# Removing the branch prefetch hints ahead of the jump over a fallback path

## The chip, the cores and the metric

The kernel runs on one core of one Trainium2 chip. The metric is the device time of one execution in microseconds. The profile's span, from the first to the last instruction, is about 1.8 us shorter than that time (342.1 us against 343.89 us for the profiled execution of the kernel before).

In the profile's lines PE is TensorE, PEld its weight loads, ACT ScalarE, DVE VectorE, POOL GpSimd and SP SyncE; a "q" behind the name means the engine's instruction sequencer, and L706 is line 706 of the kernel.

## The reference

The reference computes two independent problems A and B of attention with a cached K and V and concatenates their results. Each has 16 batches, 32 query tokens, 32 query heads on 4 key/value heads and 512 cached keys:

```python
q = (x @ wq).reshape(B, Sq, Hq, Dh)...            # 512 x 1024 times 1024 x 4096
scores = einsum("bhqd,bhkd->bhqk", q, k) * (Dh ** -0.5)
p = softmax(scores, axis=-1)
o = einsum("bhqk,bhkd->bhqd", p, v)
a = o.reshape(B, Sq, Hq * Dh) @ wo                # and b the same with the B inputs
return concatenate([a, b], axis=-1)
```

## The kernel before

The fast path takes the softmax with a constant shift in place of each row's maximum. That is good only while all row sums stay in a safe range, so VectorE counts at the end how many sums do. Every engine loads that count into a register and, if it is too small, runs a slower general path that recomputes everything. On the given inputs the count is full: **the general path is never executed, and every engine jumps over it.**

```python
            run(units, 40)                      # 40 steps of the last output projections
            tc.mark_branch_hint_location(       # what the change removes
                "general", "LikelyTaken",
                [nc.sync.engine, nc.scalar.engine, nc.vector.engine, nc.tensor.engine, nc.gpsimd.engine],
            )
            ok = nc.values_load(ok_i[0:1, 0:1], ...)      # line 670: one register load per engine
            run(units, 1 << 20)                 # the rest of the output projections
            return ok
    ...
    ok = fast_path(ok_i)
    with tc.If(ok < total, preferred_fallthrough_block=True, label="general"):   # line 679
        general_path(tc, problems, out_flat)
```

The program that this builds has, for each engine, the fast path, a compare-and-branch, then the general path (578 instructions on ScalarE, 844 on VectorE, 266 on GpSimd, 7,811 on PE, one on SyncE), then a short else block of semaphore updates, then the closing barriers. The branch is taken, to the else block. The last output piece is cast by ScalarE and stored by a DMA that ScalarE issues:

```python
                yield from f_units(1, TT - 1, 0, NW, nc.sync)
                yield from f_units(1, TT - 1, NW, QW, nc.sync)
                yield from f_units(1, TT - 1, NW + QW, QW, nc.scalar)   # the last piece
```

## Time and profile before

| | before |
|---|---|
| time, median (lowest to highest) of the first 3 runs | 343.97 us (343.52 to 344.53) |
| span of the profiled execution | 342.1 us |
| PE busy | 338.1 us |
| start of the last cast; from there to the end | 339.09 us; 3.0 us |

The page of the profile gives the span, the engines' busy times and the chain of work that ended last:

```profile
span 342.1 us, 5510 instructions
PE 338.1 (99%) x2128; PEld 214.6 (63%) x2128; DVE 265.6 (78%) x336; ACT 185.7 (54%) x209; POOL 46.6 (14%) x206
...
PE 99%; ACT 0%; issue 0%; ACTq 0%
```

TensorE bounds the kernel. The windows view splits the span where the last cast starts. The columns are the stretch, its length, the busy time of PE, PEld, DVE, ACT and POOL, the granted clock, the DMA share and GB/s; the last stretch was asked for 0.1 us past the end of the span:

```profile
0.00:339.09 339.09, 338.08 (x2128) 214.64 (x2128) 265.55 (x336) 185.35 (x208) 46.65 (x206) 1.00 0.87 211
339.09:342.20 3.11, 0.00 (x0) 0.00 (x0) 0.00 (x0) 0.37 (x1) 0.00 (x0) 1.00 0.08 24
```

The last 3 us hold one cast and nothing else that counts as busy. The hints themselves appear in the view of the kernel's last source line, to which the compiler attributes them (duration in ns as minimum/median/maximum, then the start of the first and the last in us):

```profile
L706 POOLq BRANCH_PREFETCH_HINT  x1: 56/56/56, 0.7 to 0.7; - x1
L706 ACTq BRANCH_PREFETCH_HINT  x1: 50/50/50, 0.7 to 0.7; - x1
L706 SPq BRANCH_PREFETCH_HINT  x1: 60/60/60, 0.7 to 0.7; - x1
L706 DVEq BRANCH_PREFETCH_HINT  x1: 51/51/51, 0.8 to 0.8; - x1
L706 PEldq BRANCH_PREFETCH_HINT  x1: 50/50/50, 0.8 to 0.8; - x1
```

They run at 0.7 to 0.8 us, at the very start, though the source marks them near the end. The branches appear in the view of the If's line. An engine's EVENT_SEMAPHORE on that line is its first instruction behind the jump:

```profile
L679 POOLq EVENT_SEMAPHORE  x5: 17/43/43, 331.0 to 331.4; - x5
L679 POOLq COMPARE_BRANCH  x1: 64/64/64, 330.6 to 330.6; - x1
L679 DVEq COMPARE_BRANCH  x1: 84/84/84, 330.6 to 330.6; - x1
L679 DVEq EVENT_SEMAPHORE  x1: 21/21/21, 331.2 to 331.2; - x1
...
L679 PEldq COMPARE_BRANCH  x1: 402/402/402, 336.9 to 336.9; - x1
L679 PEldq EVENT_SEMAPHORE  x1: 51/51/51, 339.1 to 339.1; - x1
L679 ACTq COMPARE_BRANCH  x1: 68/68/68, 339.9 to 339.9; - x1
L679 ACTq EVENT_SEMAPHORE  x1: 17/17/17, 340.4 to 340.4; - x1
```

ScalarE is the last to branch, at 339.9, and goes on half a microsecond later. GpSimd and VectorE have branched 9 us earlier. SyncE closes the program: it waits for all engines and stores. Its own waits on the kernel's last line, from 335 us on (what it waited for, us in total, times, longest):

```profile
...
SPq L706 <- DMA out_dram<-o_sb: 2.0, 1, 2.0
SPq L706 <- PEq L679: 1.9, 1, 1.9
...
```

Its last long wait ended when the last store landed. ScalarE's part of the job was done by then.

### The profile page before, as it was taken

What the parts mean: (1) busy time and instruction counts of PE and PEld (TensorE: products, weight loads), DVE (VectorE), ACT (ScalarE), POOL (GpSimd) and SP (SyncE); (2) the same over time, 40 slices, a digit from 0 to 9 for tenths busy, and PEclk for the clock granted to TensorE, in tenths of its full rate; (3) what the DMA queues carried; (4) which work ended last, traced back from release to release, by engine and by line L of the source; (5) the groups of instructions that cost most, each with busy time, mean ns of one, the idle gap of its engine ahead of it and who ended that gap; (6) DMA issues with size and microseconds to landing.
All of it is one profiled execution on the core that took longest, in us unless ns stands there. A gap on an engine that the chain in (4) does not pass through costs nothing.

```text
span 342.1 us, 5510 instructions
## 1 busy us (share of the span) xinstructions
PE 338.1 (99%) x2128; PEld 214.6 (63%) x2128; DVE 265.6 (78%) x336; ACT 185.7 (54%) x209; POOL 46.6 (14%) x206
## 2 busy tenths in 40 slices
PE   8999999999999999999999999999999999999996
PEld 7456666666666666666666666666666666666555
DVE  1047988888888889888888888798888888889540
ACT  2067666676666666676655554555454555555110
POOL 0001111101111111111101212222122100111100
DMA  6999999899999998999999856999439996430001
GB/s 194 253 243 183 284 261 256 173 232 269 299 234 248 238 252 231 251 304 303 281 319 259 191 125 180 283 323 211 129 104 306 350 194 139 103 96 17 17 17 33
DMA packets 128093, 71.70 MB, mean 210 GB/s; under 512 B 75840, under 2 KB 127296, under 8 KB 128064
## 3 DMA queue, kind: packets, MB, share of 16 engines
q1 hardware_dynamic: 127536, 70.21, 84.7%
q0 software_dynamic: 384, 1.05, 0.9%
q8 instruction: 17, 0.28, 0.3%
q14 instruction: 12, 0.10, 0.1%
q10 hardware_dynamic: 144, 0.07, 0.1%
HBM read 50.86 MB, written 2.10 MB: 155 GB/s over the span
## 4 chain that ended last, share of the span: by engine, by line
PE 99%; ACT 0%; issue 0%; ACTq 0%
PE f_ps L320 32%; PE q_ps L301 28%; PE ob L425 16%; PE s_ps L357 16%; PE q_ps L533 4%; PE q_ps L515 1%; PE xT_ps L523 0%; ACT o_sb L329 0%; ACTq L329 0%
## 5 line engine op out<-in xcount | busy, mean ns | idle before, releaser
L365 ACT ACTIVATE p_sb<-s_ps,shift 128x1024 bf16<-128x1024 f32 x128 | 142.6, 1114 | 97.8 <-PE s_ps L357 82.0
L376 DVE TRANSPOSE_TENSOR_REDUCE parts<-p_sb 128x32 f32<-128x1024 bf16 x128 | 158.8, 1240 | 19.2 <-ACT p_sb L365 17.6
L320 PE MATMUL f_ps<-wo_sb,oT 128*128 128x512 bf16 (+1 forms) x544 | 131.8, 366 | 0.0
L301 PE MATMUL q_ps<-xT,wq_sb 128*128 128x512 bf16 x448 | 117.4, 379 | 0.0
L425 PE MATMUL ob<-p_sb,v_sb 128*128 128x256 bf16 x512 | 76.8, 273 | 0.0
L357 PE MATMUL s_ps<-qT,kT 128*128 128x256 bf16 x512 | 76.8, 273 | 0.0
L320 PEld LDWEIGHTS <-oT 128*128 128x128 bf16 x544 | 53.2, 98 | 35.8
L357 PEld LDWEIGHTS <-kT 128*128 128x128 bf16 x512 | 56.9, 113 | 28.3
L301 PEld LDWEIGHTS <-wq_sb 128*128 128x128 bf16 x448 | 43.8, 98 | 31.7 <-DMA wq_sb<-in_A_wq_dram 0.2
L425 PEld LDWEIGHTS <-v_sb 128*128 128x128 bf16 x512 | 50.1, 98 | 20.0
L447 DVE TENSOR_TENSOR oT<-r,ob 128x512 bf16<-128x512 f32 x64 | 43.9, 686 | 21.9 <-PE ob L425 20.8
L411 DVE STREAM_TRANSPOSE r<-rall 128x512 f32<-128x512 f32 x64 | 44.2, 691 | 1.1
L309 ACT CAST qT<-q_ps 128x512 bf16<-128x512 f32 x56 | 32.6, 583 | 15.4 <-PE q_ps L301 15.4
L394 POOL COPY half<-cs 64x32 f32<-64x32 f32 x32 | 6.5, 204 | 227.4 <-DVE cs L384 227.3
L329 ACT CAST o_sb<-f_ps 128x512 bf16<-128x512 f32 (+1 forms) x17 | 9.5, 558 | 24.6 <-PE f_ps L320 24.6
L533 PE MATMUL q_ps<-xT,w_sb 128*128 128x512 bf16 (+1 forms) x70 | 15.4, 377 | 0.0
L384 DVE TENSOR_REDUCE cs<-parts 128x32 f32<-128x128 f32 x32 | 12.0, 376 | 1.1
L406 DVE RECIPROCAL rall<-sums 128x32 f32<-128x32 f32 x32 | 10.2, 320 | 3.3 <-POOL sums L403 3.3
L533 PEld LDWEIGHTS <-w_sb 128*128 128x128 bf16 x70 | 7.2, 104 | 6.9
L561 DVE CAST qT<-q_ps 128x512 bf16<-128x512 f32 x4 | 2.5, 683 | 10.2 <-PE q_ps L533 10.2
L331 POOL DMA_DIRECT2D out_dram<-o_sb x8 | 4.6, 574 | 34.7 <-ACT o_sb L329 34.6
L395 POOL TENSOR_TENSOR half<-half,cs 64x32 f32<-64x32 f32 x32 | 7.8, 242 | 2.6
(25 smaller groups left out, 46.3 us busy)
## 6 DMA issues: line engine op xcount, KB each, us to landing
v_sb<-in_A_v_cache_dram SPq DMA_DIRECT2D x16, 512.0 KB, 6.5
wq_sb<-in_B_wq_dram SPq DMA_DIRECT2D x8, 1024.0 KB, 6.0
wo_sb<-in_A_wo_dram SPq DMA_DIRECT2D x8, 1024.0 KB, 6.4
v_sb<-in_B_v_cache_dram SPq DMA_DIRECT2D x16, 512.0 KB, 4.4
wo_sb<-in_B_wo_dram SPq DMA_DIRECT2D x8, 1024.0 KB, 8.4
wq_sb<-in_A_wq_dram SPq DMA_DIRECT2D x5, 1024.0 KB, 6.3
wq_sb<-in_A_wq_dram SPq DMA_DIRECT2D x2, 512.0 KB, 5.8
kT<-in_A_k_cache_dram SPq DMA_TRANSPOSE x64, 4.5
```

What stands on the lines that cost most here:

```text
L301: nc.tensor.matmul(ps[:], lhsT=w[:, dc, (h % 4) * DH:(h % 4 + 1) * DH], rhs=xT[pr][:, dc, :], start=(dc == 0), stop=(dc == DC - 1),)
L309: nc.scalar.copy(out=qT[pr, g][:, :, hl, :], in_=ps[:].rearrange("p (b s) -> p b s", s=SQ),)
L320: nc.tensor.matmul(ps[:, 0:width], lhsT=oT[pr, tt][:, h, :], rhs=wo_tiles[pr, nh, h // REP][:, h % REP, off:off + width], start=(h == 0), ...
L357: nc.tensor.matmul(s_ps[:, c, :], lhsT=kT[:, i % GRP, c, :], rhs=qT[pr, g][:, b, :, :].rearrange("p h s -> p (h s)"), start=True, stop=True,)
L365: nc.scalar.activation(out=p_sb[:], in_=s_ps[:], func=ACTF.Exp, bias=shift[:], scale=SCALE)
L376: nc.vector.tensor_reduce(out=parts[k][:, q, :, :].rearrange("p c h -> p (c h)"), in_=st[i]["p"][:].rearrange("p c (h s) -> p (c h) s", s=SQ),
L384: nc.vector.tensor_reduce(out=cs[:], in_=parts.pop(k)[:].rearrange("p q c h -> p q h c"), axis=AX.X, op=ALU.add,)
L406: nc.vector.reciprocal(out=rall[:, k, :], in_=quad.pop(k)[:])
L411: nc.vector.transpose(out=r[:].rearrange("p n s -> p (n s)"), in_=rall[:, k, o * 2 * REP:(o + 1) * 2 * REP] .unsqueeze(2).to_broadcast([P, ...
L425: nc.tensor.matmul(ob[j][:, q, :], lhsT=v_sb[:, i % GRP, c, :], rhs=st[i]["p"][:, c, :], start=(c == 0), stop=(c == KC - 1),)
L447: nc.vector.tensor_tensor(out=out, in0=rcp.pop(j)[:].rearrange("p (q h) s -> p q h s", h=REP), in1=ob.pop(j)[:].rearrange("p q (h s) -> p ...
L533: nc.tensor.matmul(first_q[h][:, ts], lhsT=w0[dc // HC][:, dc % HC, h * DH:(h + 1) * DH], rhs=xT[0][:, dc, ts], start=(dc == 0 and t0 == 0 ...
```

## The change

By its name a hint is to have the instructions at the jump's target fetched before the jump. The change takes all five away. Its whole text is:

```diff
             run(units, 40)
-            tc.mark_branch_hint_location(
-                "general",
-                "LikelyTaken",
-                [nc.sync.engine, nc.scalar.engine, nc.vector.engine, nc.tensor.engine, nc.gpsimd.engine],
-            )
             ok = nc.values_load(ok_i[0:1, 0:1], min_val=0, max_val=total,
```

## The prediction

> **What bounds the kernel.** TensorE. The profile page gives PE 338.1 us busy of a 342.1 us span, and the chain that ended last is 99% PE. The windows view of 339.10 to 342.20 shows no PE work at all: the last 3 us are a tail in which ScalarE casts the last output piece (339.09, 0.37 us), issues its output DMA (339.49, 0.38 us), takes the compare-and-branch over the general path (339.90) and meets the other engines in the closing barriers (last record 342.05). The change touches only this tail and the kernel's first microsecond.
>
> **What the change removes.** One BRANCH_PREFETCH_HINT per engine. By the records of the kernel's last source line they do not stand where the source marks them but at 0.70 to 0.82 us, 50 to 60 ns each, ahead of SyncE's first load (0.857) and PE's first matmul (0.93). Removing them starts both some 0.06 to 0.1 us earlier: about -0.07 us.
>
> **What it adds.** The program's branch is taken (the data passes the check), over a general path of 578 ScalarE, 844 VectorE, 266 GpSimd and 7,811 PE instructions, but one SyncE instruction. [...] The trace of before[...]: from the start of the branch to the next instruction take 0.49 us (GpSimd 330.55 to 331.05), 0.61 (VectorE), 0.48 (ScalarE 339.90 to 340.39), 0.20 (SyncE), and the instruction-fetch records come only after that, 0.60 to 0.62 us after the first target instruction (331.67, 331.83, 340.98). So the targets were already there, which I put down to the hints[...].
>
> Without hints each of the four engines must fetch at the branch. Estimate from these records: about 0.1 us to decide, 0.6 to 0.9 us until the fetch starts, 0.55 us for an 8 KB fetch (PE: 16 KB, 1.1 us), [...]0.4 us to resume: about 2.2 to 2.5 us, so 1.7 to 2 us more than now; I allow 1.2 to 3.
>
> **How much is on the critical path.** GpSimd and VectorE branch at 330.6: 10 us of slack, nothing. PE's sequencer branches at 336.90 and then waits for its own matmuls until 339.05: a 2.5 to 4 us stall gives 339.4 to 340.9, still before the end. [...] ScalarE's branch counts: its end event moves from 340.40 to about 342.2. SyncE now goes on at 341.14, released by the landing of the last output DMA, so about 0.7 us of the stall is hidden behind that transfer; the rest delays the closing barriers one for one. Net: +1.8 - 0.7 - 0.07, about +1.1 us, with +0.3 to +2.6 possible.
>
> **Predicted time.** 345.1 us, range 344.2 to 346.6. Chances: faster by over 2% 0.01, within 2% 0.97, slower by over 2% 0.02.
>
> **What would show it.** No hint records at 0.7 us. In the records of the If line, the gap from ScalarE's COMPARE_BRANCH to its next event grows from 0.48 to about 2.3 us; likewise VectorE and GpSimd, not SyncE. Two instruction fetches after each branch, the first before the engine resumes. SyncE's last wait of the tail is released by ScalarE, not by the output DMA. PE's busy time unchanged at 338.1; the span grows by as much as the time.
>
> **What would make it wrong.** A fetch quick enough to hide in the 0.7 us (then no change); a hint that never worked, the target being present for another reason (then -0.07); a PE stall over 4 us, PE then ending last; or a run-to-run spread (343.52 to 344.53 before) that covers it.

Four things are cut from it, as no trace of this case shows them: a rule for when a jump has to wait for its target, with the words that refer to it; how the hints were thought to have had the targets ready; one term of the stall's estimate, which rests on no record; and where SyncE's target lies. The stall came to 2.2 to 2.5 us in the author's sum. The terms as first written add up to 1.95 to 2.25 us, and those that are left to 1.65 to 1.95 us.

## The result, and the profile after

| | before | after |
|---|---|---|
| time, median (lowest to highest) of 6 runs each | 343.94 us (343.42 to 344.53) | 345.06 us (344.70 to 346.21) |
| ratio, 95% interval | | 1.0037 (1.0019 to 1.0055) |
| span of the profiled execution | 342.1 us | 344.4 us |
| PE busy | 338.1 us | 338.5 us |
| start of the last cast; from there to the end | 339.09; 3.0 us | 339.68; 4.7 us |

A ratio is the mean time of one kernel's fast runs over that of the other's of the same rounds, so it is not quite the ratio of the medians. Here the means are 345.16 and 343.89 us, a difference of 1.27 us. The verdict at 2% is "same"; at this resolution the kernel is slower by about a third of a per cent. The profiled execution of after was the slowest of its six.

The windows view of after, split at its last cast:

```profile
0.00:339.68 339.68, 338.46 (x2128) 214.75 (x2128) 265.53 (x336) 185.34 (x208) 46.66 (x206) 1.00 0.87 211
339.68:344.50 4.82, 0.00 (x0) 0.00 (x0) 0.00 (x0) 0.37 (x1) 0.00 (x0) 1.00 0.07 20
```

Of the 2.3 us by which this span is longer, 0.6 lie ahead of the last cast and 1.7 behind it. Part of the 0.6 has nothing to do with the branch: PE waited 0.4 us for a late weight tile at 72 us, as it does for 0.2 to 0.8 us in the traces of e4, e6, e7 and e9. The If's line in after (five source lines higher, as the call is gone):

```profile
L674 POOLq EVENT_SEMAPHORE  x5: 17/43/43, 333.7 to 334.1; - x5
L674 POOLq COMPARE_BRANCH  x1: 45/45/45, 331.1 to 331.1; - x1
L674 DVEq COMPARE_BRANCH  x1: 72/72/72, 331.2 to 331.2; - x1
...
L674 DVEq EVENT_SEMAPHORE  x1: 21/21/21, 334.2 to 334.2; - x1
...
L674 PEldq COMPARE_BRANCH  x1: 3335/3335/3335, 337.5 to 337.5; - x1
L674 ACTq COMPARE_BRANCH  x1: 54/54/54, 340.5 to 340.5; - x1
L674 PEldq EVENT_SEMAPHORE  x1: 51/51/51, 340.9 to 340.9; - x1
L674 ACTq EVENT_SEMAPHORE  x1: 17/17/17, 343.4 to 343.4; - x1
```

Four engines now stand still for 2.6 to 3.3 us at the branch. On PE the stall is inside the branch's own record (3,335 ns against 402); on the others it is the gap behind it. SyncE's waits from 335 us on:

```profile
SPq L701 <- PEq L674: 3.2, 1, 3.2
SPq L701 <- ACTq L674: 2.5, 1, 2.5
...
```

SyncE is now released by ScalarE (ACTq) and no longer by the store. To the nanosecond, from the raw instruction and fetch records of the two traces (us from the span's start):

```
                                       before      after
ScalarE issues the last store          339.494     340.085
ScalarE compare-and-branch             339.904     340.497
fetch of instructions starts, length      -        341.703, 0.307
ScalarE's first instruction behind it  340.388     343.432
last store landed, SyncE sees it       341.141     341.735
SyncE sees ScalarE's event (wait ends) 341.169     343.478
last instruction ends                  342.104     344.411
```

In before, ScalarE's event (it ends at 340.405) comes 0.74 us ahead of the landing. In after, its event (343.449) comes 1.71 us behind the landing. The branch gap grew from 0.484 to 2.935 us, that is by 2.45 us; 0.74 us of it is hidden behind the store, and 1.71 us stick out. That is the whole growth of the tail.

### The profile page after: what moved, and what is told of

It is laid out like the page before. It is cut to its first block, busy times and chain, and to the rows that moved or that the text cites. A ratio compares the mean times of both kernels' runs of the same rounds, so it can differ in the third digit from the quotient of the medians.

```text
span 344.4 us, 5505 instructions
## 1 busy us (share of the span) xinstructions
PE 338.5 (98%) x2128; PEld 214.8 (62%) x2128; DVE 265.5 (77%) x336; ACT 185.7 (54%) x209; POOL 46.7 (14%) x206
## 4 chain that ended last, share of the span: by engine, by line
PE 90%; SPq 6%; DMA 2%; issue 0%; ACT 0%; ACTq 0%
PE f_ps L320 32%; PE q_ps L301 23%; PE ob L425 15%; PE s_ps L357 15%; PE q_ps L533 4%; SPq L275 3%; DMA wq_sb<-in_A_wq_dram 2%; SPq L602 2%; PE q_ps L515 1%; PE xT_ps L523 0%; SPq L283 0%; SPq L246 0%; ACT o_sb L329 0%; ACTq L329 0%
```

## The experiments

The theories, as they stood before the runs:

- **S**: only ScalarE's stall reaches the end, because ScalarE issues the last store and branches last. Rival **P**: PE's stall, the longest, sets the end.
- **W**: the stall is the fetch of a target that is far from the branch; a near one needs none. Rival **F**: any taken branch without a hint pays a flat penalty. Rival **B**: for ScalarE a target behind half of the general path (289 or 290 instructions) is still near. Rival **M**: the stall belongs to a conditional branch gone the wrong way.
- **O**: the stall costs what sticks out past the landing of the last store, and no more.

Kernels are compared only within the same rounds.

"Gap" is the time from the start of an engine's branch to the start of its next instruction, from the raw records. "Tail" is the time from the start of ScalarE's last cast to the end of the span. Before has a tail of 3.01 us, after 4.73 us. All these kernels gave correct results.

### e1: ScalarE's hint alone

```diff
-                [nc.sync.engine, nc.scalar.engine, nc.vector.engine, nc.tensor.engine, nc.gpsimd.engine],
+                [nc.scalar.engine],
```

> Only ScalarE keeps its hint. Theory S (ScalarE's stall at the branch, 2.94 us in the trace of after against 0.48 before, is all that reaches the end): ScalarE's branch gap back to 0.4 to 0.5 us; PE's branch record stays 3.3 us long, VectorE and GpSimd gaps about 3.0 and 2.6 us, all hidden; SyncE's last wait released by the output DMA again; first load at 0.74 us as in after. Time 343.7, that is before minus 0.1 to 0.2 us. Rival P (PE's stall, the longest, 3.3 us, sets the end): time stays about 1.1 us above before, 345.1.

Measured: ratio 0.9995 (0.9982 to 1.0008); median 343.59 us against 343.57 for before. The tail is 3.01 us. From the view of the If's line:

```profile
L679 PEldq COMPARE_BRANCH  x1: 3318/3318/3318, 336.6 to 336.6; - x1
L679 ACTq COMPARE_BRANCH  x1: 68/68/68, 339.6 to 339.6; - x1
L679 PEldq EVENT_SEMAPHORE  x1: 51/51/51, 340.0 to 340.0; - x1
L679 ACTq EVENT_SEMAPHORE  x1: 17/17/17, 340.1 to 340.1; - x1
```

PE stalls 3.3 us, GpSimd and VectorE 2.62 and 2.97 us, and it costs nothing: the tail is that of before to 0.01 us. ScalarE's hint is worth all that the five are worth.

### e2: all hints but ScalarE's

```diff
+                [nc.sync.engine, nc.vector.engine, nc.tensor.engine, nc.gpsimd.engine],
```

> All engines but ScalarE keep the hint. Theory S: ScalarE's gap about 2.9 us, the other four as before, first load at 0.86 us as before; time 1.2 to 1.7 us above before, 345.3 (a little over after, since the hints' issue slots at the start are paid and nothing is gained). Rival P: time as before, 343.9.

Measured: ratio 1.0045 (1.0031 to 1.0058), means 1.55 us apart; tail 4.58 us; ScalarE's gap 2.79 us, the others as in before (0.49, 0.61, 0.20 us, PE's record 402 ns). SyncE's longest wait:

```profile
SPq L706 <- ACTq L679: 3.6, 1, 3.6
```

With e1 this settles S against P for this layout of the program. PE is not far behind, though: in e1 it comes out of its branch at 339.95 us, 0.9 us ahead of the landing of the last store. Here the growth of the tail (1.57 us) and the difference of the means (1.55 us) agree.

### e3 and e4: half of the general path, and a stub of it, without hints

None of e3 to e6 is a correct kernel for all inputs, as the fallback is incomplete; all give correct results on these, where it isn't executed.

```diff
 # e3
-        general_path(tc, problems, out_flat)
+        general_path(tc, problems[:1], out_flat)
 # e4: the same, and eight loops inside general_path cut to one or two turns
```

> No hints; the general path (never executed on these inputs) handles one problem only: 290 ScalarE, 424 VectorE, 134 GpSimd, 3,907 PE instructions to jump over instead of 578, 844, 266, 7,811. Theory W[...]: GpSimd's [...]gap drops to about 0.5 us with no fetch before it resumes; ScalarE, VectorE and PE still stall 2.9, 3.0 and 3.3 us; time as after, 345.1. Rival F (any taken branch without a hint pays a flat penalty): GpSimd's gap stays 2.6 us. Rival B[...]: ScalarE's gap drops to 0.5 us as well and the time falls to 343.7.

> No hints; the general path cut to a stub (9 ScalarE, 14 VectorE, 19 GpSimd, 92 PE instructions), never executed on these inputs. Theory W: [...]no stall: gaps 0.2 to 0.6 us on all five, PE's branch record about 0.4 us, no target fetch; time before minus 0.1 to 0.2 us, 343.7. Rival F (flat penalty of an unhinted taken branch): gaps and time as after, 345.1.

Measured: e3 1.0115 (1.0100 to 1.0129), 3.9 us slower; e4 1.0027 (1.0014 to 1.0041), 0.9 us slower. Both times missed what was expected, e3's by far. The gaps did as theory W says: in e3 GpSimd 0.47, VectorE 2.93, ScalarE 2.56 us; in e4 GpSimd 0.18, VectorE 0.23, ScalarE 0.39, SyncE 0.19 us, PE's record 363 ns. What spoiled the times was the build. As the cut general path no longer writes problem B's part of the output, nothing ties the last store to the If, and the framework's builder put it behind the If (e5 and e6, whose stub still writes that part, kept it ahead). The timeline of ScalarE in e3 shows it:

```profile
338.72 0.37 ACT L329 CAST o_sb<-f_ps 128x256 bf16<-128x256 f32 x1 [3.12 <-PE f_ps L320]
341.43 2.06 ACTq L331 DMA_DIRECT2D out_dram<-o_sb  x1
```

The store now comes 2.7 us behind the start of the cast (0.40 in before), as it has to sit through the stall, and issuing it takes 2.06 us in place of 0.38, with one more instruction fetch inside (at 341.88 us). The tail is 7.0 us. In e4 the store slid behind the If too, but without a stall there, and the tail is 3.12 us. The rest of e4's 0.9 us lies ahead of the tail; in its trace PE waits 0.3 and 0.2 us for late tiles of v and wq. Why its six runs have more of that than others stays open.

### e5: half of the general path, the store kept in place

```diff
-        general_path(tc, problems, out_flat)
+        general_path(tc, problems[1:], out_flat)
```

> As e3, but the never executed general path keeps the problem whose output piece is stored last, so that store should stay ahead of the branch (in e3 it had slid behind it and cost time of its own). 289 ScalarE, 137 GpSimd, 3,907 PE instructions to jump over. Theory W: GpSimd's gap 0.5 us without a fetch first, ScalarE's 2.6 to 2.9 us with one, PE's record 3.3 to 3.7 us; time as after, 1.1 to 1.5 us above before. Rival B[...]: ScalarE's gap 0.5 us, time at most as before.

Measured: ratio 1.0034 (1.0014 to 1.0054), means 1.10 us apart; tail 4.65 us; gaps GpSimd 0.47, VectorE 2.83, ScalarE 2.86 us. From the view of the If's line:

```profile
L674 POOLq EVENT_SEMAPHORE  x5: 17/43/43, 330.3 to 330.6; - x5
L674 POOLq COMPARE_BRANCH  x1: 45/45/45, 329.8 to 329.8; - x1
...
L674 ACTq COMPARE_BRANCH  x1: 54/54/54, 339.1 to 339.1; - x1
...
L674 ACTq EVENT_SEMAPHORE  x1: 17/17/17, 342.0 to 342.0; - x1
```

In one and the same program, an unhinted taken branch over 137 instructions (GpSimd) takes half a microsecond and one over 289 (ScalarE) takes 2.9. These are two engines, but GpSimd alone says the same: over 266 instructions, in after, it took 2.59 us. So the distance matters, not the missing hint as such: F falls. B falls too: behind 289 instructions ScalarE's target was not near (2.86 us). Where between 8 and 289 instructions the limit lies for ScalarE was not measured.

### e6: a stub, the store kept in place

Edit: as e5, and eight loops of the general path cut to one or two turns (8 ScalarE, 19 VectorE, 30 GpSimd, 104 PE instructions).

> As e4, with the store of the last piece kept ahead of the branch: stub of 8 ScalarE, 19 VectorE, 30 GpSimd, 104 PE instructions. Theory W: no stall on any engine (gaps 0.1 to 0.4 us), SyncE's last wait released by the output DMA; from the last cast to the end 3.0 us as in before (4.7 in after); time 0 to 0.3 us under before. Rival F (flat penalty of an unhinted taken branch): ScalarE's gap 2.9 us, 4.7 us from the last cast to the end, time as after.

Measured: ratio 1.0004 (0.9982 to 1.0027); tail 2.98 us; gaps 0.18, 0.23, 0.19 and 0.19 us on GpSimd, VectorE, ScalarE and SyncE, and 363 ns for PE's record. No instruction fetch of GpSimd, VectorE or ScalarE follows the branches. SyncE's longest wait is for the store again:

```profile
SPq L701 <- DMA out_dram<-o_sb: 2.0, 1, 2.0
```

Without any hint, but with a near target, the tail is that of before. The 0 to 0.3 us under before that were expected don't show.

### e7: the last store issued by SyncE, no hints

```diff
-                yield from f_units(1, TT - 1, NW + QW, QW, nc.scalar)
+                yield from f_units(1, TT - 1, NW + QW, QW, nc.sync)
```

> No hints, full general path; the last output piece is stored by SyncE instead of ScalarE. Theory O (the stall costs only what sticks out past the landing of the last store): ScalarE's sequencer can take the branch as soon as its last cast is dispatched, 0.8 us earlier against that cast than in after, its stall stays 2.6 to 2.9 us, so the end comes 3.9 to 4.0 us after the start of the last cast instead of 4.7; time 0.6 to 0.8 us under after, 0.3 to 0.8 above before. Rival: the stall's length is what counts, wherever it starts: time as after.

Measured: ratio 1.0003 (0.9984 to 1.0022), means 0.28 us apart; tail 3.43 us. ScalarE's sequencer takes the branch 0.01 us after the start of the cast, against 0.81 us in after; its stall is 2.44 us; its event comes 0.4 us behind the landing of the store. The wait that is left for SyncE:

```profile
SPq L701 <- ACTq L674: 0.8, 1, 0.8
```

This bears O out. The expected tail (3.9 to 4.0 us) was too long, as the stall came out shorter than the 2.6 us assumed. It is 0.5 us shorter than in after, and it starts 0.8 us earlier against the cast, beside the issue and flight of the store, and the tail shrinks by 1.3 us: 0.8 for the earlier start and 0.5 for a shorter stall. This kernel needs no hint and comes within noise of before.

### e8: the else block placed first, no hints

```diff
-    with tc.If(ok < total, preferred_fallthrough_block=True, label="general"):
+    with tc.If(ok < total, preferred_fallthrough_block=False, label="general"):
```

> No hints, the If laid out so that the short else block falls through; that block then jumps over the general path to the end. Theory W: the compare-and-branch costs ScalarE 0.1 to 0.5 us and its end event comes at once, but the jump behind it stalls just the same (2.5 to 2.9 us until its drain), since its target is as far away: 4.5 to 4.7 us from the last cast to the end; time as after, 1.1 to 1.5 us above before. Rival M (the stall belongs to a mispredicted conditional branch): no stall, time 0 to 0.3 us under before.

Measured: ratio 1.0047 (1.0026 to 1.0069), means 1.57 us apart; tail 4.84 us. Each engine now has two branches; the second is the jump from the else block to the end.

```profile
L674 PEldq COMPARE_BRANCH  x2: 91/1931/3771, 336.4 to 338.7; - x2
L674 ACTq COMPARE_BRANCH  x2: 38/46/53, 339.4 to 339.6; - x2
...
L674 ACTq EVENT_SEMAPHORE  x1: 17/17/17, 339.5 to 339.5; - x1
```

And from the view of the kernel's last line, ScalarE's drain at the end:

```profile
L701 ACTq DRAIN  x2: 8/37/66, 342.2 to 342.8; - x2
```

The first, conditional one falls through in 0.10 us; PE's takes 91 ns. The second stalls: ScalarE's next instruction, its drain, comes at 342.24, 2.68 us later, and PE's record is 3,771 ns long. So M falls: it doesn't matter whether the branch that is far is the conditional one. Laying the If out the other way only moves the far jump. Two things were not expected, and with them the tail and the time came out a little above what was forecast (4.7 and 1.5 us). First, the last store took 3.1 us to land (1.6 in before and after). A 16 KB instruction fetch, taken for PE's (only one queue moves 16,384 bytes at a time, 17 times in before, where PE has 4,267 of the 5,510 recorded instructions), ran at 339.77 to 341.14, at the same time as that store (issued at 338.98), and the last eight packets of the store ran only from 341.13 on. That the two got into each other's way was not shown. Second, in this layout it is PE that ends last (a line of SyncE's waits, then one of the view of the kernel's last line):

```profile
SPq L701 <- PEq L701: 1.0, 2, 0.5
L701 PEldq DRAIN  x2: 8/40/73, 342.5 to 342.9; - x2
```

In after PE's far branch stood ahead of its wait for its own matmuls and began at 337.5; here the far jump stands behind that wait and begins at 338.69. PE's drain comes at 342.51, 0.3 us behind ScalarE's (342.24) and 0.4 behind the landing of the store (342.13). So which engine's stall sets the end depends on where its jump stands.

### e9, e10, e11: the small gain at the start

e9 is e1 again, e10 is after again; e11 takes away SyncE's hint alone:

```diff
+                [nc.scalar.engine, nc.vector.engine, nc.tensor.engine, nc.gpsimd.engine],
```

> The kernel of e1 once more, to see whether it beats before. ScalarE's hint alone should give the tail of before (3.0 us from the last cast to the end) with SyncE's first load at 0.74 instead of 0.86 us: 0.1 to 0.3 us under before, if the loads' own spread (0.5 us between runs) lets it be seen.

> The changed kernel once more, on the chip of e9 and e11: 4.6 to 4.8 us from the last cast to the end again (before: 3.0), whatever the loads do ahead of it; first load at 0.74 us; time 1.2 to 1.5 us over before, 1.4 to 1.7 over e9.

> All hints but SyncE's[...]. Branch gaps of all five as in before, 3.0 us from the last cast to the end; first load at 0.74 us as in after while PE still starts at 0.93. If what the hints cost at the start is SyncE's slot, time as e9; if PE's slot matters too, between e9 and before.

| | median us | ratio to before, 95% interval | tail us | first load at us |
|---|---|---|---|---|
| before, same rounds | 343.58 | | 3.01 (first trace) | 0.86 |
| e9, ScalarE's hint alone | 343.65 | 0.9993 (0.9979 to 1.0007) | 3.01 | 0.74 |
| e10, no hints (after) | 344.69 | 1.0028 (1.0015 to 1.0042) | 4.65 | 0.74 |
| e11, all hints but SyncE's | 343.40 | 0.9990 (0.9977 to 1.0004) | 3.02 | 0.74 |

The tails came as expected and the times of e10 lower than expected (0.98 us over before and 0.72 over e9 by the means, where 1.2 to 1.5 and 1.4 to 1.7 had been forecast). Two of e9's seven runs took 344.9 and 345.0 us, so that by the plain means of all runs it lies 0.27 us above before, though its ratio over the same rounds is below 1. Whether dropping the hints of engines that don't need them gains the 0.1 to 0.3 us that e9 was to show can't be told: all three intervals (e1, e9, e11) hold 1. No version was found that clearly beats both kernels.

## Why the prediction was right

- **The time.** Predicted 345.1 us (344.2 to 346.6); measured 345.06 us, and 344.69 us when repeated in e10. The mechanism was right; that the number agrees to 0.04 us is luck, as the mis-sized terms below show.
- **Which engine counts.** Predicted: ScalarE's branch only. Shown by e1 and e2: with its hint alone the tail is 3.01 us, with all hints but its own 4.58 us. The other three stalls are real (2.6, 3.0, 3.3 us in after) and hidden, as predicted. SyncE's gap was unchanged (0.20 and 0.19 us), as predicted.
- **Why it stalls.** Predicted: the target must be fetched at the branch. Shown by e5 and e6, where only the distance changed: over 8 instructions 0.19 us on ScalarE, over 289 2.86 us, over 578 2.94 us; and by an instruction fetch that starts and ends inside ScalarE's gap in every trace where that gap is long. In after it starts at 341.70 us, 1.21 us behind the start of the branch, and ends 1.42 us ahead of the next instruction.
- **The hidden part.** Predicted: about 0.7 us of ScalarE's stall disappears behind the landing of the last store. Measured: 0.74 us. Confirmed by e7, which hides more of it.
- **A term that was mis-sized: the stall.** It was put at 2.2 to 2.5 us; it is 2.94 us in after and 2.86 in e10. The terms as written add up to 1.95 to 2.25 us, without the one that is cut to 1.65 to 1.95 us. The transfer was about right (0.31 us in after, 0.68 in e5; put at 0.55). Too small were the ends: from ScalarE's branch to the start of the fetch 0.92 to 1.25 us over the traces (put at 0.7 to 1.0), and from the end of the fetch to the next instruction 1.08 to 1.42 us (put at 0.4 by the term that is left, at 0.7 with the cut one). So the tail grew by 1.72 us and not by 1.1.
- **The other mis-sized term: the start.** It was put at -0.07 us. SyncE's first load starts 0.12 us earlier (0.74 against 0.86) and PE 0.15 us earlier (0.78 against 0.93). The time of after grew by 0.45 us less than its tail (1.27 against 1.72), that of e10 by 0.66 us less (0.98 against 1.64). These two errors of the estimate have opposite signs, and that is why its sum came out so well. Where the 0.45 to 0.66 us come from is not settled. It may be noise: e6 and e7 start without hints too, and their time grew by 0.14 us more and by 0.14 us less than their tail. The start of the last cast lay anywhere between 338.3 and 340.2 us in the 13 traces, as PE waited for some late tile or not; e11, which moves only the first load, came out 0.29 us under before by the means, with a ratio whose interval holds 1.
- **How the hint had done it.** The records show this much: in before no 8 KB instruction fetch stands between the one that starts at 289.1 us and the first branch at 330.6 us, and yet GpSimd, VectorE and ScalarE were at their next instruction 0.48 to 0.61 us after the branch, ahead of any such fetch (331.67, 331.83 and 340.98 us). In the two traces with SyncE's hint (before and e2) there are 9 fetches of 8 KB between 5 and 325 us; in the other 11 there are 10, the tenth at 307 to 310 us. Which fetch belongs to which engine is not recorded, so how the targets came to be there stays open.

## What to carry to other kernels

Here a taken branch over a long block of code cost 2.4 to 3.0 us on the engine that took it (3.3 to 3.8 on PE) unless a hint stood at the start: with one it took 0.48 to 0.61 us on GpSimd, VectorE and ScalarE, though the hint (a record of 50 to 60 ns at 0.7 to 0.8 us) lay 330 to 339 us back. But a kernel pays only for the engine that comes out of its branch last (ScalarE here, PE in e8), and only for what sticks out past the last store's landing. So find that engine first; hint it, or let it branch before the last store by issuing that store elsewhere, or keep its share of the skipped code short (137 instructions were short enough on GpSimd, 266 were not). An experiment that shortens code which is never executed can still move instructions that are: look at the build before trusting its time.
